# Two exchanges in the load queue of a causal-attention and feed-forward kernel on one core

## The chip, the cores and the metric

The kernel runs on one core of one Trainium2 chip. The metric is the device time of one execution in microseconds (us). The kernel before was run three times. The profile is of one further execution, and all times inside it count from the start of its span. The span goes from the first to the last instruction of the program; the device time is a little longer than the span.

## The reference

Inputs are q, k, v of shape (4 batches, 8 heads, 768 positions, 64), one decay factor lam for each head, and two float64 weight matrices: w_in (512 x 2048) and w_out (2048 x 512). The first half is linear attention with decay, in blocks of 64 positions:

```python
intra = einsum('bhic,bhjc->bhij', qb, kb) * Dmask      # Dmask: lam ** (i - j) for i >= j, else 0
intra = einsum('bhij,bhjd->bhid', intra, vb)
inter = einsum('bhid,bhde->bhie', qb * lam_pow, kv_state)
out[:, :, sl] = intra + inter
kv_state = lam_block * kv_state + einsum('bhsd,bhse->bhde', kb * rev_pow, vb)
```

The attention output, 3072 tokens of 512 features, goes through the second half:

```python
h = x @ w_in
g = maximum(0.01 * h, h)
return (g @ w_out).astype(float32)
```

## The kernel before

**Tiling.** The 3072 tokens are 24 chunks of 128 positions (6 chunks for each batch, two blocks of 64 in each chunk), and 4 chunks make a group of 512 tokens. The 2048 hidden features are 8 pairs of 2 x 128. For each group and each pair the kernel does an up projection (line 864) with its leaky ReLU on ScalarE (line 891), and stores the result to a scratch in DRAM (line 894). After the last group the down projection reads this scratch back (line 904) and multiplies by w_out (line 930). Each operand of these products is split into three float32r parts (h, l, m), and each product is made of three matmuls.

**One chunk of attention.** `load_kq` loads k and q, each in two DMAs of 128 KB (line 476), and `load_v` loads v in one DMA of 256 KB (line 538); both walk rows of 64 float32 numbers. `transposes` turns k and q with four TensorE transposes each (line 560), and ScalarE or VectorE copies them out of PSUM (line 541). k is then scaled in place by the decay (line 601). `scores` makes the kv products, which need k and v of the chunk, and the scores q k^T, with small 64 x 64 matmuls (line 420; in the trace they write psc, or banks called pt and b in the first four chunks). `outputs` makes scores times v and the first half of the inter-block product (48 small matmuls into po), then a tiny copy of two columns of po, called seen_po (line 692), then the scores of the next chunk, then the other half of the inter-block product (16 small matmuls into po). Those last 16 wait for seen_po. Then ScalarE writes the h part of the output (line 708) and VectorE the l and m parts (lines 716 and 734).

From chunk 8 on q is not transposed by TensorE: it is loaded in 16 blocks that are already put in place for VectorE's 32 x 32 transposes (`load_subs`, line 523, 32 KB for each block of chunks 8 and 9; `turn`, line 532).

**The weights.** `to_float32` loads half a pair of w_in as float64 words into one of three raw buffers, in two DMAs of 256 KB with rows of 2048 bytes (line 798), and makes float32 of it: three ScalarE instructions (lines 810, 812 and 814) and two of VectorE (lines 816 and 817). `parts` splits the pair into its parts wh, wm and wl (lines 823, 826 and 828).

**What sets the order.** Each step is recorded with `add` in a `Plan`, with its engine, a cost and the buffers that it reads and writes; it gets a number in the order of recording. `ORDER` (line 266) is a list of (number, engine) written out by hand, 1296 entries, that says in which order the recorded steps are emitted. Each engine then takes its own instructions in that order, and so does SyncE, which issues the loads one after the other. `Plan.emit` works out waits from the buffers that each step reads and writes.

```python
for i, e in self.order:
    if i < 0:
        done.append((free[e], len(done), i, e))
        free[e] -= 0.11 * i
        continue
    take(max(free[e], since(i, e)), i, e)
```

(A negative number asks for filler matmuls at that place; those stand early in the list.) Loads use few buffers: k, q and v have two each, taken by even and odd chunks, with extra places for chunks 2 and 3 (in buffers called gs and raw), and w_in rotates through three raw buffers.

The marker that orders the two halves of the inter-block product is recorded like this, and `ORDER` puts the one of chunk 7 on ScalarE, as (309, "ACT"):

```python
add(("DVE", "ACT"), (0.15, 0.25), lambda e: (nc.vector.tensor_copy if e == "DVE" else nc.scalar.copy)(seen_po, po[:, :, 0, 0]),
    ["po"], ["seen_po"], rank=-3.0)
between()
add("PE", 0.235, lambda: inter(1), needs + ["seen_po"], ["po"], kind="q")
```

The numbers that the change touches are 74 (load of v of chunk 3), 111 (two loads of q of chunk 4), 355 (two loads of w_in, second half of pair 7), 275 (one block of q for chunks 8 and 9) and 303 (load of v of chunk 8). The three conversions of the w_in half stand in ScalarE's order directly ahead of marker 309.

Of the kernel before, what the change touches and what calls it, by code (L numbers as in the profile page):

```python
# [239 lines left out]
def kernel(  # L240
# [127 lines left out]
    plan = Plan(kinds, also, {"k@2": early[0], "v@2": early[0], "k@3": early[1], "v@3": early[1], "q@3": early[2]})  # L368
    plan.fill, plan.idle, plan.warm, plan.order = busy, None if ORDER else busy, 1.3 + 0.22 * WARM, ORDER
    add = plan.add  # L370
# [686 lines left out]
```

## Time and profile before

| what | us |
|---|---|
| three runs | 608.04, 606.27, 607.43 |
| median | 607.43 |
| the profiled execution | 606.49 |
| its span | 604.7 |
| TensorE matmul busy | 595.9 |
| TensorE weight loads busy | 492.0 |
| VectorE busy | 294.4 |
| ScalarE busy | 209.2 |
| GpSimd busy | 70.0 |

In the profile PE is TensorE's matmuls, PEld its weight loads, DVE VectorE, ACT ScalarE, POOL GpSimd, and SPq SyncE's queue, which issues the loads. A row of the timeline has the start, the length, the engine, the line of the kernel, the operation, and what it writes and reads (att, gs, raw, po and so on are the names of the tiles; in_q_dram and the like are the inputs); a bracket at its end tells how long the engine was idle before it and what released it. A row of the waits has who waited for what, the sum, how often, and the longest. The length of an issue in SyncE's queue is not the time of the transfer: the landing comes later and has its own row, in us from issue to landing. The ends of matmuls are modelled, so a short wait can hide behind them.

### The profile page before, as it was taken

Reading aid. Unit: us, or ns where it says so; the run is one execution under the profiler, and the core shown is the slowest. Engines: PE = TensorE matmul, PEld = TensorE weight load, DVE = VectorE, ACT = ScalarE, POOL = GpSimd, SP = SyncE. Lnnn points to the kernel's source line nnn. Section 1 sums busy time; section 2 is a strip of 40 time slices with the busy share of each in tenths; the row PEclk is TensorE's granted clock in tenths of the full one; section 3 lists DMA queues with packets and bytes.
Section 4 is the critical chain, followed back from the end, with each engine's and each line's share of the span. In section 5 each row is a group of like instructions: output and inputs, shape, how many; then the busy total and the mean of one; then the engine's idle time right before and its main releaser. Section 6 shows DMA issues by size and latency. Waiting matters only on the chain.

```text
span 604.7 us, 12740 instructions
## 1 busy us (share of the span) xinstructions
PE 595.9 (99%) x5362; PEld 492.0 (81%) x5362; DVE 294.4 (49%) x410; ACT 209.2 (35%) x323; POOL 70.0 (12%) x84
## 2 busy tenths in 40 slices
PE   8899999999999999999999999999999999999997
PEld 5788888888888888887888888888888888888886
DVE  6798754450554434244167755354353543534430
ACT  4686651212433433435334421222312313214111
POOL 2311232241322031140000000000000000000000
PEclk9999999999999999999999999999999999999999
DMA  9998887597788788664975823433333333423201
GB/s 208 226 266 224 224 241 199 88 258 188 214 227 210 224 241 232 183 203 181 327 258 184 302 105 128 151 99 134 116 116 128 118 126 122 125 102 124 85 1 69
DMA packets 150249, 105.18 MB, mean 174 GB/s; under 512 B 126128, under 2 KB 126896, under 8 KB 150192
## 3 DMA queue, kind: packets, MB, share of 16 engines
q1 hardware_dynamic: 148848, 104.03, 58.6%
q8 instruction: 42, 0.69, 0.5%
q10 hardware_dynamic: 1344, 0.33, 0.2%
q14 instruction: 15, 0.12, 0.1%
HBM read 68.69 MB, written 35.65 MB: 173 GB/s over the span
## 4 chain that ended last, share of the span: by engine, by line
PE 95%; DMA 2%; SPq 1%; issue 0%; ACT 0%; DVE 0%; DVEq 0%; ACTq 0%
PE b L864 32%; PE b L930 16%; PE pt L864 11%; PE psc L930 11%; PE po L930 11%; PE pt L930 5%; PE po L420 4%; PE psc L420 3%; DMA att<-in_v_dram 2%; DMA att<-in_q_dram 1%; PE b L560 0%; PE po L560 0%; SPq L798 0%; PE b L420 0%; PE b L359 0%
## 5 line engine op out<-in xcount | busy, mean ns | idle before, releaser
L912 DVE SCALAR_TENSOR_TENSOR xl<-att,xh 128x1024 fp32r<-128x1024 f32 x48 | 58.7, 1223 | 125.8 <-ACT xh L911 125.8
L911 ACT ACTIVATE xh<-att 128x1024 fp32r<-128x1024 f32 x48 | 50.9, 1061 | 147.5 <-PE po L930 73.0
L864 PE MATMUL b<-xl,wl 128*128 128x512 f32 (+1 forms) x292 | 77.1, 388 | 0.0
L864 PE MATMUL b<-xh,wh 128*128 128x512 f32 (+1 forms) x292 | 76.5, 389 | 0.6 <-ACT wh L823 0.6
L864 PE MATMUL b<-xm,wm 128*128 128x512 f32 (+1 forms) x292 | 76.0, 390 | 0.0
L891 ACT ACTIVATE gs<-b 128x512 f32<-128x512 f32 x72 | 42.1, 597 | 96.3 <-PE b L864 87.1
L864 PEld LDWEIGHTS b<-xh,wh 128*128 128x128 f32 x292 | 53.9, 188 | 11.8 <-ACT wh L823 0.7
L864 PEld LDWEIGHTS b<-xl,wl 128*128 128x128 f32 x292 | 54.1, 188 | 11.2
L864 PEld LDWEIGHTS b<-xm,wm 128*128 128x128 f32 x292 | 53.8, 188 | 11.2
L914 DVE SCALAR_TENSOR_TENSOR xm<-xl,xh 128x1024 fp32r<-128x1024 f32 x48 | 58.8, 1226 | 4.7
L930 PE MATMUL b<-wh,xh 128*128 128x512 f32 x144 | 56.0, 389 | 0.0
L930 PE MATMUL b<-wl,xl 128*128 128x512 f32 x144 | 56.0, 389 | 0.0
L930 PE MATMUL b<-wm,xm 128*128 128x512 f32 x144 | 56.0, 389 | 0.0
L663 POOL TENSOR_TENSOR att<-att 128x256 f32<-128x256 f32 x40 | 27.8, 694 | 113.9 <-DVE att L660 66.2
L930 PE MATMUL psc<-wm,xm 128*128 128x512 f32 (+1 forms) x100 | 38.2, 387 | 0.0
L930 PE MATMUL po<-wm,xm 128*128 128x512 f32 (+1 forms) x100 | 37.9, 384 | 0.0
L930 PE MATMUL psc<-wh,xh 128*128 128x512 f32 x96 | 37.3, 389 | 0.0
L930 PE MATMUL psc<-wl,xl 128*128 128x512 f32 x96 | 37.3, 389 | 0.0
L930 PE MATMUL po<-wh,xh 128*128 128x512 f32 x96 | 37.3, 389 | 0.0
L930 PE MATMUL po<-wl,xl 128*128 128x512 f32 x96 | 37.3, 389 | 0.0
L420 PEld LDWEIGHTS po<-att 64*64 64x64 f32 x1408 | 27.0, 134 | 10.5 <-issue 7.8
L420 PE MATMUL po<-att 64*64 64x64 f32 x1408 | 33.0, 222 | 1.7 <-issue 0.9
(106 smaller groups left out, 860.5 us busy)
## 6 DMA issues: line engine op xcount, KB each, us to landing
att<-g SPq DMA_DIRECT2D x48, 512.0 KB, 3.4
g<-gs SPq DMA_DIRECT2D x47, 512.0 KB, 3.6
raw<-in_moe_w_in_dram SPq DMA_DIRECT2D x32, 256.0 KB, 4.3
raw<-in_moe_w_out_dram SPq DMA_DIRECT2D x16, 512.0 KB, 4.6
out_dram<-gs SPq DMA_DIRECT2D x23, 256.0 KB, 2.1
att<-in_v_dram SPq DMA_DIRECT2D x22, 256.0 KB, 3.8
att<-in_k_dram SPq DMA_DIRECT2D x43, 128.0 KB, 3.9
wo<-w SPq DMA_DIRECT2D x8, 512.0 KB, 4.0
```

Of the source, the lines that this page charges most:

```text
L420: nc.tensor.matmul(dst[HALF[cols]], lhsT=lhsT[HALF[rows]], rhs=rhs[HALF[rows]], start=start, stop=True, skip_group_check=True)
L663: add("POOL", 0.62, lambda new=new, j=j: behind(("s", j), nc.gpsimd.tensor_tensor(state[(j + 1) % 4], new, _bc(lam_c, 2, D), op=ALU.mult)) ...
L864: nc.tensor.matmul(dst, lhsT=w[z][:, kk * 2 * P + f * P:kk * 2 * P + (f + 1) * P], rhs=x[z][:, kk, toks], start=start and kk == 0, stop=kk ...
L891: add("ACT", ns, lambda b=b, r=r: nc.scalar.activation(out=r(), in_=b(), func=AF.Prelu, bias=0.0, scale=1.0, alpha=0.01), [kb], [kg], rank ...
L911: add("ACT", 1.05, lambda: nc.scalar.activation(out=h, in_=graw[j], func=AF.Copy, bias=0.0, scale=NEAR), reads, wr("h"))
L912: add("DVE", 1.215, lambda: nc.vector.scalar_tensor_tensor(l, graw[j], 1.0, h.bitcast(F32), op0=ALU.mult, op1=ALU.subtract), reads + [f"rh ...
L914: add("DVE", 1.215, lambda: nc.vector.scalar_tensor_tensor(m, l.bitcast(F32), -S, h.bitcast(F32), op0=ALU.mult, op1=ALU.add), [f"rh{j}", f ...
L930: nc.tensor.matmul(to[:, cols], lhsT=ring[j][z][:, f * T + tb * P:f * T + (tb + 1) * P], rhs=W[pp][z][:, f * d_model:(f + 1) * d_model][:, ...
```

## The change

Only the list `ORDER` is changed. The entry of q of chunk 4 (111) moves nine places forward, to stand just ahead of v of chunk 3 (74). Further on, v of chunk 8 (303) moves forward past the w_in load (355), and the q block (275) with it, so that the three go out as 303, 275, 355 where they went out as 355, 275, 303. The diff, cut to the entries about it (the list is one line in the code):

```diff
-    (98, "ACT"), (44, "ACT"), (74, "DMA"), (41, "POOL"), (45, "PE"), (54, "ACT"), (55, "DVE"),
-    (99, "DVE"), (100, "DVE"), (75, "PE"), (57, "DVE"), (111, "DMA"), (58, "PE"), (46, "ACT"),
+    (98, "ACT"), (44, "ACT"), (111, "DMA"), (74, "DMA"), (41, "POOL"), (45, "PE"), (54, "ACT"),
+    (55, "DVE"), (99, "DVE"), (100, "DVE"), (75, "PE"), (57, "DVE"), (58, "PE"), (46, "ACT"),
...
-    (282, "DMA"), (304, "DMA"), (355, "DMA"), (288, "ACT"), (275, "DMA"), (207, "POOL"),
+    (282, "DMA"), (304, "DMA"), (303, "DMA"), (275, "DMA"), (355, "DMA"), (288, "ACT"), (207, "POOL"),
...
-    (439, "DVE"), (293, "DVE"), (303, "DMA"), (357, "ACT"), (300, "POOL"),
+    (439, "DVE"), (293, "DVE"), (357, "ACT"), (300, "POOL"),
```

In SyncE's queue, which is the only one whose order changes, this reads (each line one step, "x2" for two DMAs):

```diff
 L798 raw<-in_moe_w_in_dram x2
+L476 att<-in_q_dram x2
 L538 gs<-in_v_dram
-L476 att<-in_q_dram x2
 L798 raw<-in_moe_w_in_dram x2
...
 L476 att<-in_k_dram x2
-L798 raw<-in_moe_w_in_dram x2
-L523 att<-in_q_dram
 L538 att<-in_v_dram
+L523 att<-in_q_dram
+L798 raw<-in_moe_w_in_dram x2
 L894 g<-gs
```

2 lines of the change are left out of this document (1 added, 1 removed).

## The prediction

> **What bounds the kernel now.** I read the page first, then the waits of TensorE, then its order of time around the places that those waits name, then the chain of work that ended last, and last the load queue and ScalarE at the same places.
>
> ```profile
> span 604.7 us, 12740 instructions
> ...
> PE 595.9 (99%) x5362; PEld 492.0 (81%) x5362; DVE 294.4 (49%) x410; ACT 209.2 (35%) x323; POOL 70.0 (12%) x84
> ```
>
> TensorE is busy 595.9 of 604.7 us, so 8.8 us is all that any reordering could win without making TensorE's work shorter, and this change does not touch that work. TensorE's waits name both places of the change:
>
> ```profile
> PE b L560 <- DMA att<-in_q_dram: 0.6, 1, 0.6
> ...
> PE psc L420 <- DMA att<-in_v_dram: 0.5, 1, 0.5
> ```
>
> The first is the transpose of q of chunk 4, the second the kv product of chunk 8. Together they are 1.1 us. The rest of the span is told by three stretches (columns: stretch, its length, busy time of PE, PEld, DVE, ACT, POOL, clock, DMA share, GB/s):
>
> ```profile
> 20.00:42.00 22.00, 20.77 (x452) 17.99 (x455) 19.30 (x33) 15.17 (x28) 6.17 (x7) 1.00 1.00 258
> ...
> 66.00:70.00 4.00, 3.47 (x137) 2.99 (x135) 2.62 (x6) 2.71 (x6) 1.06 (x1) 1.00 0.99 310
> 70.00:604.70 534.70, 531.27 (x4094) 439.62 (x4092) 238.97 (x306) 165.77 (x248) 52.01 (x56) 1.00 0.55 166
> ```
>
> From 70 us on TensorE has no listed wait, so whatever it gains or loses before 70 us arrives at the end one for one. And from 20 to 42 us the DMA engines are busy all the time (share 1.00): a load there lands when the bytes ahead of it are done, not when it was issued.
>
> **The change part by part.** No instruction is added or removed, and TensorE, VectorE, ScalarE and GpSimd keep their order. In SyncE's queue the two loads of q4 step ahead of the load of v3, and further back v8 and one block of q step ahead of the two loads of the second half of w_in of pair 7. So the cost is in landings alone.
>
> *First exchange.* TensorE at this place, the chain at the same place, and the two issues:
>
> ```profile
> 24.27 0.64 PE L864 MATMUL b<-xh,wh 128*128 128x256 f32 x4
> 25.55 0.95 PE L560 MATMUL b<-att 128*128 128x128 f32 x4 [0.64 <-DMA att<-in_q_dram]
> ...
> 26.89 0.27 PE L420 MATMUL pt<-gs 64*64 64x64 f32 x1
> ```
> ```profile
> 20.64 5.37 DMA att<-in_q_dram
> ...
> 26.05 0.44 PE b L560 x2
> ```
> ```profile
> 19.48 0.43 SPq L538 DMA_DIRECT2D gs<-in_v_dram  x1
> 20.01 1.45 SPq L476 DMA_DIRECT2D att<-in_q_dram  x2
> ```
>
> The second load of q4 lands at 20.64 + 5.37 = 26.01. TensorE loses 0.64 us before the first two transposes and, since four take 0.44 x 2 = 0.88 by the chain's row for two, under 0.3 us more before the last two: 0.9 us in all. One load of v costs the queue about 1.2 us (below, v8). Taken from ahead of q4 it lets q4 land at about 24.8, before TensorE is free at 24.91. So this wait goes. What is late next is v3: with the same bytes queued it lands where q4 did, at 26.01. Its reader is the kv product of chunk 3 (26.89), which would come at 26.89 - 0.9 = 26.0 and so starts at about 26.1. **Gain here: 0.8 us.**
>
> It does not last. The next loads are in the old order behind the same bytes, and v5 is already just in time:
>
> ```profile
> 40.56 0.86 PE po L420 x48
> 41.42 0.02 issue
> 41.44 1.09 PE psc L420 x44
> ```
> ```profile
> 36.62 0.59 SPq L538 DMA_DIRECT2D att<-in_v_dram  x1
> ```
> ```profile
> DMA to landing us min/median/max: 4.7/4.7/4.7
> ```
>
> v5 lands at 36.62 + 4.7 = 41.3; the product that reads it starts at 41.44. From v8's landing at 64.17 + 3.5 = 67.7 to its product at 67.84 it is the same 0.14 us. So at 41.44 TensorE is being let go by v5, although the list of waits shows nothing there, because the 48 matmuls ahead have modelled ends. If v5 does not land sooner, TensorE waits there for what it won at 26 us. Bounds of what survives: 0 (the landing stays) and 0.8 us (every later load moves along with TensorE). With a DMA share of 1.00 up to 42 us there is no idle DMA time to move into: I take **0**.
>
> *Second exchange.* The load queue, and behind it what each row took from issue to landing, in the same order (k9, w_in, q block, v8):
>
> ```profile
> 60.43 0.93 SPq L476 DMA_DIRECT2D att<-in_k_dram  x2
> 61.46 2.19 SPq L798 DMA_DIRECT2D raw<-in_moe_w_in_dram  x2
> 63.70 0.42 SPq L523 DMA_DIRECT2D att<-in_q_dram  x1
> 64.17 0.45 SPq L538 DMA_DIRECT2D att<-in_v_dram  x1
> ```
> ```profile
> DMA to landing us min/median/max: 3.7/3.8/3.9
> ```
> ```profile
> DMA to landing us min/median/max: 3.8/4.1/4.3
> ```
> ```profile
> DMA to landing us min/median/max: 2.8/2.8/2.8
> ```
> ```profile
> DMA to landing us min/median/max: 3.5/3.5/3.5
> ```
>
> Landings: k9's second load about 60.9 + 3.7 = 64.6; w_in 61.46 + 3.8 = 65.3 and about 62.0 + 4.3 = 66.3; the q block 66.5; v8 67.7. Their steps are 0.7, 1.0, 0.2 and 1.2 us, without a hole from 64.6 to 67.7. In the new order the same steps give v8 at 65.8, q at 66.0, w_in at 66.7 and 67.7. If 0.3 of w_in's step of 1.0 was its late issue (its twin took 0.7), it is 67.4. So v8 comes 1.9 us sooner, and **w_in 1.1 to 1.4 us later**. Who waits for w_in is ScalarE:
>
> ```profile
> 66.37 0.70 ACT L810 ACTIVATE w<-raw 128x512 f32<-128x512 f32 x1 [2.77 <-DMA raw<-in_moe_w_in_dram]
> 66.97 0.76 ACT L812 ACTIVATE low<-raw 128x512 uint16<-128x512 uint32 x1
> 67.61 0.77 ACT L814 ACTIVATE low<-raw 128x512 f16<-128x512 f32 x1
> 68.24 0.14 ACT L692 COPY att<-po 128x2 f32<-128x2 f32 x1
> 69.30 0.60 ACT L708 ACTIVATE xh<-po 128x512 fp32r<-128x512 f32 x1 [0.92 <-PE po L420]
> ```
> ```profile
> 66.38 0.93 PE L420 MATMUL po<-att 64*64 64x64 f32 x48
> 67.84 1.16 PE L420 MATMUL psc<-att 64*64 64x64 f32 x64 [0.53 <-DMA att<-in_v_dram]
> 68.79 0.44 PE L420 MATMUL po<-att 64*64 64x64 f32 x16
> ```
>
> ScalarE starts 0.07 after the landing and does three conversions in a row. Queued behind them stands the tiny copy of line 692 (the marker seen_po), and the last 16 matmuls of chunk 7, in TensorE's queue, wait for that marker. It is done at 68.38, 0.41 before those matmuls start at 68.79. Without the wait for v8 they would be ready at 68.79 - 0.53 = 68.26, so even with w_in untouched TensorE could gain only 68.79 - 68.38 = 0.41 us here. With w_in 1.1 to 1.4 later the marker ends at 69.5 to 69.8, and the 16 matmuls start 1.1 - 0.41 = 0.7 to 1.4 - 0.41 = 1.0 us later than now, some hundredths more for the release. **A wait of about 1.4 us takes the place of the 0.5 us one.** All that reads their result (line 708, the eviction, the up projection) moves along with TensorE.
>
> The Trainium skill, page "DMA: Bandwidth & Descriptors", section "Anatomy of one DMA — SWDGE (gpsimd) path", fits a DMA's moving part as bytes over 436 GB/s (for the other descriptor path). By it v8 (256 KB) and the q block (32 KB) would set w_in back by an estimated 0.7 us and the loss would be 0.3 us. The rows differ: v8's step alone is 1.2 us.
>
> *Sum.* 0 from the first exchange, 0.9 us lost at the second (between 0.7 and 1.0, rounded up for the release). The profiled execution took 606.49 us (span 604.7 and 1.8 around it), so it would be 607.4; it lies 0.94 below the median of the runs shown, 607.43. On the median the forecast is **608.3 us**.
>
> **The rivals.**
>
> *A, both waits simply go.* For it: each exchange hits a listed wait, and SyncE itself waits for TensorE now and then, so later loads may be issued sooner. Against: the full DMA engines, and the marker's place in ScalarE's order. It needs w_in's second load to land by 66.3 as now, and v5 0.8 sooner. It gives -0.8 and -0.41, about -1.2: 606.2.
>
> *B, the other way and larger: w_in's issue stalls.* One of the two w_in issues lasted 2.19 - 0.45 = 1.7 us instead of about 0.45, and landed about 2.6 after that issue ended (63.65 to 66.3). I assume that this stall stays at its time, about 62.0, where the q block is issued in the new order. If it goes with the w_in load instead, w_in's second issue ends at about 64.6 + 1.3 = 65.9 and lands near 68.5 to 68.9, 2.2 to 2.6 late: the 16 matmuls lose 1.8 to 2.2 us. It decides from an issue that ends after 65.1, as then the landing is later than the 67.7 of the queue. Against: the q block is issued first, and would take the stall. 609.4.
>
> *C, the change does not do what it says.* The gain at 26 us dies at v5, and w_in comes only a little later, by as much as the marker's slack of 0.41 or the 0.7 us of its bytes: 0 to +0.3, 607.6.
>
> **How the numbers follow.** Forecast 0.50, A 0.15, B 0.20, C 0.15. The range reaches to A and B: 606.2 to 609.6, the upper end being B's 609.4 and the 0.2 that its price is unsure of; what is left out is larger forms of A and B and a median that falls apart from this one. A median of this kernel cannot tell less than about 0.3%, 1.8 us, from no change (the three runs lie 1.8 apart). Faster by over that needs more than all the waits of A: 0.08, for A with a low median. Slower by over it: B and a few hundredths of the forecast, 0.26. Within it: 0.66.
>
> **What the profile of the changed kernel would show.** First exchange: no wait of line 560 near 25 us, the kv product of chunk 3 starting at about 26.1, and the product at 41.44 no sooner than now, with a gap before it of up to 0.8 in place of 0.02. Second: v8 landing near 66, no wait for it; ScalarE's line 810 starting at 67.5 to 67.8 in place of 66.37; the 16 po matmuls at about 69.5 to 69.8 with a listed wait for line 692. I am wrong if the product of v5 starts well before 41.4 (then the first gain survives), if line 810 starts near 66.4 (A or C), or if it starts after 68.3 (B). If the span changes with none of these moved, the cause is one that I have not seen.

## The result, and the profile after

The changed kernel took 608.24 us (median of 22 runs, 606.42 to 613.55), the kernel before 607.07 us beside it (22 runs, 606.08 to 608.91). The ratio is 1.0031, with a 95% interval of 1.0016 to 1.0046: slower by a little over 0.3%. The forecast was 608.3.

The middle hides two groups of runs. In 16 of the 22 TensorE's mean granted clock (the clock that it was given, 1.0 being full speed) is 0.999 or 1.0, and their mean time is 607.86 us. In the other six it is 0.994 to 0.997, and their mean is 612.08. The 22 runs of the kernel before have a mean of 607.07. So the difference of the means, 609.01 - 607.07 = 1.94 us, is 0.79 us in runs at full clock and 6/22 x (612.08 - 607.86) = 1.15 us from six runs at a lower clock. The profiled execution (612.42 us, span 610.6) is one of the six, so it shows both.

**First place.** TensorE's order in time in the changed kernel (start, duration, engine, line, and in brackets the idle time ahead with what ended it):

```profile
25.33 0.60 PE L560 MATMUL b<-att 128*128 128x128 f32 x4
...
26.33 0.27 PE L420 MATMUL pt<-gs 64*64 64x64 f32 x1
...
38.40 0.66 PE L560 MATMUL pt<-att 128*128 128x128 f32 x4 [0.23 <-ACT gs L891]
...
40.18 0.69 PE L560 MATMUL po<-att 128*128 128x128 f32 x4 [0.19 <-ACT low L814]
40.80 0.93 PE L420 MATMUL po<-att 64*64 64x64 f32 x48
41.96 1.09 PE L420 MATMUL psc<-att 64*64 64x64 f32 x46 [0.23 <-DMA att<-in_v_dram]
```

The same 48 matmuls (po, line 420) in the kernel before:

```profile
40.49 0.93 PE L420 MATMUL po<-att 64*64 64x64 f32 x48
```

The transposes of line 560 wait no more, and the kv product of chunk 3 starts at 26.33 in place of 26.89, 0.56 us sooner. v3, its input, lands at 20.13 + 5.9 = 26.03. One execution beside one other tells little here, though: e2, e8 and e10 below leave the first exchange out, line 560 does not wait in their profiles either, and the same product starts at 25.83, 25.99 and 25.55. The lead is gone before v5 is reached: the 48 matmuls ahead of its product start at 40.80 (40.49 before), behind the two short waits for ScalarE in the rows. The product itself starts at 41.96 (41.44 before), 0.18 us after v5's landing at 35.88 + 5.9 = 41.78.

**Second place.** The load queue (k9, v8, q block, w_in, the store of line 894), and what v8 and w_in took from issue to landing:

```profile
61.16 0.94 SPq L476 DMA_DIRECT2D att<-in_k_dram  x2
62.15 2.31 SPq L538 DMA_DIRECT2D att<-in_v_dram  x1
64.51 0.57 SPq L523 DMA_DIRECT2D att<-in_q_dram  x1
65.18 0.87 SPq L798 DMA_DIRECT2D raw<-in_moe_w_in_dram  x2
66.15 0.38 SPq L894 DMA_DIRECT2D g<-gs  x1
```
```profile
DMA to landing us min/median/max: 5.0/5.0/5.0
```
```profile
DMA to landing us min/median/max: 4.5/4.6/4.6
```

The issue that lasted long is now v8's own: 2.31 us instead of 0.45. v8 lands at 62.15 + 5.0 = 67.15, w_in near 65.6 + 4.6 = 70.2. ScalarE in the same stretch:

```profile
70.29 0.66 ACT L810 ACTIVATE w<-raw 128x512 f32<-128x512 f32 x1 [5.97 <-DMA raw<-in_moe_w_in_dram]
70.86 0.77 ACT L812 ACTIVATE low<-raw 128x512 uint16<-128x512 uint32 x1
71.49 0.75 ACT L814 ACTIVATE low<-raw 128x512 f16<-128x512 f32 x1
72.10 0.14 ACT L692 COPY att<-po 128x2 f32<-128x2 f32 x1
```

The marker of line 692 depends on nothing that is late; it merely stands behind three conversions that wait for w_in. TensorE:

```profile
67.10 0.93 PE L420 MATMUL po<-att 64*64 64x64 f32 x48
67.85 0.65 PE L420 MATMUL psc<-att 64*64 64x64 f32 x32
68.87 0.69 PE L420 MATMUL psc<-att 64*64 64x64 f32 x32 [0.38 <-DVE att L532]
72.31 0.70 PE L420 MATMUL po<-att 64*64 64x64 f32 x16 [2.74 <-ACT att L692]
72.94 2.07 PE L864 MATMUL b<-xm,wm 128*128 128x512 f32 x4
74.81 1.91 PE L864 MATMUL pt<-xh,wh 128*128 128x512 f32 x4
```

The wait for v8 is gone, and one of 2.74 us for the marker has come. The 16 matmuls start at 72.31 in place of 68.79: 0.72 us of this TensorE already brought along (67.10 against 66.38 for the 48 ahead), 2.80 are new. The next rows show a second loss: four matmuls that took 1.19 us now take 2.07. The granted clock tells why. First two stretches of the changed kernel, then the same matmuls (from the 16 to the product that starts at 80.03 after, 73.85 before) in both kernels; the columns are the stretch, its length, busy time of five engines, clock, DMA share, GB/s:

```profile
71.36:78.18 6.82, 5.87 (x28) 4.64 (x29) 5.55 (x11) 5.10 (x10) 0.00 (x0) 0.50 0.70 175
78.20:80.00 1.80, 1.80 (x9) 1.50 (x8) 1.80 (x3) 1.51 (x3) 0.39 (x1) 1.00 0.84 290
```
```profile
72.31:80.03 7.72, 7.72 (x36) 6.14 (x37) 6.97 (x11) 5.75 (x9) 0.42 (x1) 0.62 0.75 198
```
```profile
68.79:73.85 5.06, 5.06 (x52) 4.17 (x44) 4.26 (x8) 3.89 (x6) 0.00 (x0) 1.00 0.90 262
```

The clock is 0.50 from 71.36 on, still inside the wait, and 1.00 again from 78.20. The same work takes 7.72 instead of 5.06 us: 2.66 more. Then 0.72 + 2.80 + 2.66 = 6.18, which is what TensorE is behind at that point (80.03 - 73.85), and the two spans differ by 5.9.

### The profile page after: what moved, and what is told of

Read it like the earlier page. It is cut to its first block, busy times and chain, and to the rows that moved or that the text cites. A ratio compares the mean times of both kernels' runs of the same rounds, so it can differ in the third digit from the quotient of the medians.

```text
span 610.6 us, 12741 instructions
## 1 busy us (share of the span) xinstructions
PE 599.1 (98%) x5362; PEld 494.1 (81%) x5362; DVE 294.8 (48%) x410; ACT 208.5 (34%) x323; POOL 70.0 (11%) x84
## 4 chain that ended last, share of the span: by engine, by line
PE 94%; DMA 3%; SPq 1%; ACT 1%; issue 0%; DVE 0%; POOL 0%; DVEq 0%; ACTq 0%; POOLq 0%
PE b L864 31%; PE b L930 16%; PE psc L930 11%; PE po L930 11%; PE pt L864 11%; PE pt L930 5%; PE po L420 4%; PE psc L420 3%; DMA raw<-in_moe_w_in_dram 2%; DMA att<-in_v_dram 1%; PE b L359 1%; SPq L538 1%; PE b L560 0%; ACT low L812 0%; PE pt L560 0%
## 5 line engine op out<-in xcount | busy, mean ns | idle before, releaser
L663 POOL TENSOR_TENSOR att<-att 128x256 f32<-128x256 f32 x40 | 27.7, 693 | 120.6 <-DVE att L660 69.8
```

The lines of the kernel that those rows point to most:

```text
L663: add("POOL", 0.62, lambda new=new, j=j: behind(("s", j), nc.gpsimd.tensor_tensor(state[(j + 1) % 4], new, _bc(lam_c, 2, D), op=ALU.mult)) ...
```

## The experiments

The theories. **T**: the late w_in costs because ScalarE's marker stands behind the conversions of this w_in; TensorE waits there, and when the wait is long its clock is halved for some microseconds. **Rival 1**: the first exchange costs. **Rival 2**: neither place has a price, the difference is spread. **Rival 3**, formed after the first four runs: the clock halves for a cause other than the wait. In the table "low" counts runs with a mean clock below 0.998, and the ratio is to the kernel before on the same chip (35, 31, 29 and 11 runs of it beside the four sets, two of these 106 low).

| kernel | median us | before us | ratio (95%) | low |
|---|---|---|---|---|
| after | 608.24 | 607.07 | 1.0031 (1.0016 to 1.0046) | 6 of 22 |
| e1 first exchange alone | 607.01 | 607.53 | 0.9995 (0.9980 to 1.0011) | 0 of 12 |
| e2 second exchange alone | 609.44 | 607.53 | 1.0029 (1.0008 to 1.0050) | 6 of 12 |
| e3 after, conversions late | 608.74 | 607.53 | 1.0025 (1.0008 to 1.0041) | 3 of 12 |
| e4 before, conversions late | 609.57 | 607.53 | 1.0036 (1.0022 to 1.0050) | 0 of 12 |
| e5 after, also behind xm | 608.26 | 606.77 | 1.0021 (1.0007 to 1.0035) | 0 of 12 |
| e6 before, also behind xm | 608.76 | 606.77 | 1.0029 (1.0017 to 1.0042) | 1 of 7 |
| e7 after, filler in the wait | 608.41 | 606.77 | 1.0026 (1.0014 to 1.0037) | 0 of 12 |
| e8 v8 past the q block only | 607.79 | 606.77 | 1.0010 (0.9998 to 1.0022) | 0 of 11 |
| e9 after, marker and L708 first | 607.28 | 606.40 | 1.0008 (0.9997 to 1.0018) | 0 of 12 |
| e10 before, marker and L708 first | 607.93 | 606.40 | 1.0021 (1.0010 to 1.0032) | 0 of 12 |
| e11 after, conversions not waiting | 606.28 | 606.40 | 0.9987 (0.9973 to 1.0000) | 0 of 11 |
| e12 after, w_in one later | 610.93 | 606.60 | 1.0069 (1.0047 to 1.0092) | 5 of 6 |

**e1, the first exchange alone**, and **e2, the second alone** (entries of ORDER, against the kernel before):

```diff
 e1
+(111, "DMA"), (74, "DMA"), (41, "POOL"),
-(74, "DMA"), (41, "POOL"),
...
-(57, "DVE"), (111, "DMA"), (58, "PE"),
+(57, "DVE"), (58, "PE"),
 e2
-(304, "DMA"), (355, "DMA"), (288, "ACT"), (275, "DMA"),
+(304, "DMA"), (303, "DMA"), (275, "DMA"), (355, "DMA"), (288, "ACT"),
...
-(293, "DVE"), (303, "DMA"), (357, "ACT"),
+(293, "DVE"), (357, "ACT"),
```

> The first exchange alone (q of chunk 4 ahead of v of chunk 3). Theory (the whole loss sits behind the late w_in load): no change, -0.3 to +0.3 us; the transposes near 25 us no longer wait, and by the product of v5 near 41.4 us TensorE is where it was. Rival 1 (the first exchange costs, since in the changed kernel's trace TensorE is 0.5 us later at that product): +0.5 to +1.2 us.

> The second exchange alone (v of chunk 8 and the q block ahead of w_in). Theory: the whole loss, +0.9 to +1.5 us in the median; line 810 on ScalarE starts 1.1 us or more later, the last 16 po matmuls of chunk 7 wait 1.4 us or more for line 692, and some executions, those with the longest wait, are 4 us and more slower with a lower granted clock. Rival 1: at most +0.3 us. Rival 2 (no price in the queue, the spread of the changed kernel is only noise): within 0.3 us and no wider spread than before.

The first alone cannot be told from no change; the second alone is as slow as the whole change, within its interval. e1's interval reaches up to 0.7 us, so a small price of the first exchange is not excluded by it alone; but the second is slow without the first, and Rival 1 is out as the cause. The profiled execution of e2 (606.64 us, clock 1.0) shows the new wait by itself; first TensorE, then ScalarE:

```profile
65.36 0.93 PE L420 MATMUL po<-att 64*64 64x64 f32 x48
66.11 1.11 PE L420 MATMUL psc<-att 64*64 64x64 f32 x64
68.65 0.46 PE L420 MATMUL po<-att 64*64 64x64 f32 x16 [1.43 <-ACT att L692]
69.04 1.20 PE L864 MATMUL b<-xm,wm 128*128 128x512 f32 x4
```
```profile
66.62 0.68 ACT L810 ACTIVATE w<-raw 128x512 f32<-128x512 f32 x1 [4.04 <-DMA raw<-in_moe_w_in_dram]
...
68.45 0.13 ACT L692 COPY att<-po 128x2 f32<-128x2 f32 x1
```

No wait for v8, and 1.43 us for the marker. Here the clock stays whole; in six other runs of this kernel it does not, and their median is 610.97 against 607.34 of the rest. The rest have a mean of 607.53, no more than the 607.46 of the kernel before beside them: in these 12 runs the loss is all in the six with a low clock, and the length of the wait by itself is not seen in the times.

**e3 and e4, the conversions late.** To take the marker from behind the conversions, these were moved behind the marker, behind L708 and behind the evictions that follow, with and without the exchanges; the two VectorE steps that go on with them (359, 360) went along:

```diff
-(352, "ACT"), (296, "POOL"), (356, "ACT"), (341, "PE"),
+(352, "ACT"), (296, "POOL"), (341, "PE"),
...
-(357, "ACT"),
...
-(358, "ACT"),
...
-(309, "ACT"), (359, "DVE"),
+(309, "ACT"),
...
-(313, "ACT"), (400, "DMA"), (342, "PE"), (360, "DVE"), (314, "DVE"), (198, "DVE"),
+(313, "ACT"), (342, "PE"), (264, "ACT"), (343, "ACT"), (347, "ACT"), (356, "ACT"), (357, "ACT"), (358, "ACT"), (400, "DMA"),
+(314, "DVE"), (359, "DVE"), (360, "DVE"), (198, "DVE"),
```

> Both exchanges, and ScalarE's three conversions of that half of w_in (with the two steps of VectorE behind them) put behind line 692, line 708 and the three evictions. Theory: the wait for line 692 goes and v8 no longer waits, so 0.3 to 0.7 us faster than before, with a narrow spread and the clock at 1.0. Rival 1: still +0.5 to +1.2 us slower. Rival 2: as the changed kernel.

> The kernel before with the same move on ScalarE and VectorE and no exchange of loads. Theory: v8 still lands late, so the wait of 0.5 us stays and the time is that of before, -0.2 to +0.3 us; it tells whether the move itself is worth anything. Rival 2: the same.

T's numbers were missed, in e4 too: 2.0 us over the kernel before, where -0.2 to +0.3 was expected. The marker's wait is gone in e3, but a row stands in its list of waits (us in total, times, longest) that no theory had:

```profile
PE b L864 <- DVE xm L734: 1.0, 1, 1.0
```

The move put 359 and 360 ahead of step 198 on VectorE, the xm part of chunk 7 (L734), so that xm now waited for the late conversions instead of the marker; e4 has the same wait. A repair that passes a wait on to the next queue is no test of T. What can be read from the pair is that with the marker out of the way the exchanges show no loss: 608.74 against 609.57. Why three runs of e3 still had a low clock its one profile (clock 1.0) does not show.

**e5 and e6, 359 and 360 behind xm as well.**

```diff
-(314, "DVE"), (359, "DVE"), (360, "DVE"), (198, "DVE"), (354, "DVE"), (294, "DVE"),
+(314, "DVE"), (198, "DVE"), (354, "DVE"), (294, "DVE"),
...
-(147, "DVE"),
+(147, "DVE"), (359, "DVE"), (360, "DVE"),
```

> Both exchanges; in ScalarE's list the three w_in conversions (L810, L812, L814) stand behind the marker L692, behind L708 and the three ScalarE steps that follow it; on VectorE their two followers now stand behind the xm step (L734) and three more, so that xm is not held as it was in e3. Theory T (the late w_in costs only because ScalarE's marker and then xm stand behind its conversions, and the long wait then halves TensorE's clock): no wait for L692, no wait of L864 for xm, every run at a granted clock of 0.999 or more, 606.5 to 607.6, no run above 609.5. Rival 2 (the exchanges have no price there, the difference is spread): no change against the kernel after, 608.2. Rival 3 (the clock halves for another cause, not for the wait at the marker): runs at 0.994 to 0.997 stay, a quarter of all, with times above 609.5.

> The same move of the conversions without the two exchanges, so that the move's own price is seen. T: 607.0 to 608.0, all runs at 0.999 or more; the wait for v8 (0.5 us) stays, so it is 0 to 0.8 us slower than e5. Rival 2: equal to e5 within 0.3 us. Rival 3: as T says here.

No wait for L692 or xm, and no run of e5 has a low clock, as T said; its time, 608.26, is not what T said, and neither is the 608.76 of e6. Rows of e5, TensorE and ScalarE:

```profile
66.10 1.16 PE L420 MATMUL psc<-att 64*64 64x64 f32 x64
67.08 0.41 PE L420 MATMUL po<-att 64*64 64x64 f32 x16
...
80.35 2.23 PE L864 MATMUL b<-xh,wh 128*128 128x512 f32 x8 [0.84 <-ACT gs L891]
```
```profile
75.19 0.79 ACT L812 ACTIVATE low<-raw 128x512 uint16<-128x512 uint32 x1 [1.66 <-DMA raw<-in_moe_w_in_dram]
...
79.70 0.60 ACT L891 ACTIVATE gs<-b 128x512 f32<-128x512 f32 x1 [1.94 <-DMA g<-gs]
```

The 16 matmuls follow without a gap. But the conversions now end at 71.6, the w_in buffers come free later, and the next w_in conversion starts at 75.19 (73.20 before). SyncE, whose next four issues of w_in need these buffers, spends 7.84 us on them (3.39 before), so the store of line 894 behind them goes out at 76.81 (74.42 before). The eviction at 79.70 waits until this store has landed, and TensorE at 80.35 waits for the eviction. e6 has the same wait, 0.91 us. So the move itself costs, and only the pair can be compared.

**e7, filler.** Three matmuls without use (six records in the trace) in front of the 16, so that TensorE is not idle while it waits:

```diff
-(406, "DMA"), (312, "PE"),
+(406, "DMA"), (-18, "PE"), (312, "PE"),
```

> Both exchanges, and in TensorE's list three matmuls of an identity (512, 512 and 128 columns, some 1.9 us at the full clock, their result unused) directly ahead of the 16 po matmuls that wait for the marker. The wait itself is not touched, only the idleness in it. T: no run under a granted clock of 0.998, so none of the times of 609.8 to 613.6 that six of 22 runs of the kernel after had; the usual wait of about 1.4 us is overfilled by 0.5 us, so the median is 607.8 to 608.9. Rival 3 (clock halves for another cause): a quarter of the runs stay at 0.994 to 0.997 and the median rises to 608.7 or more. Rival 2: median 608.2 + 0.5 to 1.9.

Three rows of TensorE and one of ScalarE:

```profile
66.51 1.11 PE L420 MATMUL psc<-att 64*64 64x64 f32 x64
67.55 2.21 PE L359 MATMUL pt<-att 128*128 128x512 f32 x6
69.69 0.46 PE L420 MATMUL po<-att 64*64 64x64 f32 x16
```
```profile
68.70 0.13 ACT L692 COPY att<-po 128x2 f32<-128x2 f32 x1
```

In this execution the filler outlasts the wait (the marker is there at 68.83, the 16 start at 69.69), so the median is no better. But none of 12 runs has a low clock, against 6 of 22 and 6 of 12 without filler: that speaks for the idle time as what halves the clock. (These 12 ran on another chip than e2, and the kernel after was not run beside them.) Rival 3 comes up again with e12 below.

**e8, v8 past the q block only**, still behind w_in:

```diff
-(355, "DMA"), (288, "ACT"), (275, "DMA"),
+(355, "DMA"), (288, "ACT"), (303, "DMA"), (275, "DMA"),
```

> Of the second exchange only the harmless half, and the first exchange not at all: v of chunk 8 goes ahead of the block of q, both stay behind the w_in load. v8 then lands about 0.2 us earlier (the q block's step), w_in is not set back. T: 607.0 to 607.8, as the kernel before; no run under 0.999; at most 0.2 us of the wait for v8 gone, the q block 1.2 us later, at 67.7. Rival 2: the same. Rival 3 (any earlier v8 halves the clock): runs at 0.997 or below appear.

No low clock appears. 607.79 lies inside the expected 607.0 to 607.8, but it is 1.02 us over the kernel before beside it, and the interval only just includes no change. Two rows of its profile:

```profile
67.75 0.69 PE L420 MATMUL psc<-att 64*64 64x64 f32 x32 [1.19 <-DMA att<-in_v_dram]
69.18 0.69 PE L420 MATMUL psc<-att 64*64 64x64 f32 x32 [0.74 <-DVE att L532]
```

v8 came no sooner in this execution: it landed at 63.44 + 4.2 = 67.6 (67.7 before). The q block behind it landed at 63.91 + 3.9 = 67.8 instead of 66.5, and half of the scores waited once more for VectorE, which turns this block (line 532). So the q block is not harmless there, and e8 does not tell what a sooner v8 costs.

**e9 and e10, conversions directly behind the marker and L708**, ahead of the evictions:

```diff
+(313, "ACT"), (356, "ACT"), (357, "ACT"), (358, "ACT"), (400, "DMA"),
...
+(147, "DVE"), (359, "DVE"), (360, "DVE"),
```

> Both exchanges; the three w_in conversions stand directly behind the marker L692 and behind L708 in ScalarE's list (in e5 they stood behind three evictions L891 more), their VectorE followers behind the xm step as in e5. Theory T (the price of the late w_in is the marker's place behind its conversions; the price left in e5 is a w_in buffer that comes free late, so that the next w_in loads wait, 75.19 in place of 73.20 for the next conversion): no wait for L692 and none for xm, all runs at a granted clock of 0.999 or more; the conversions start near 68.1 instead of 69.6, so the loss behind it is 0.5 to 1.5 us smaller than in e5: 0 to 1 us over the kernel before, and 0.5 to 1.0 under the same move without exchanges (e10). Rival 2 (no price in the queue): equal to e5 and to e10 within 0.3 us. Rival 3 (clock halves for another cause): runs at 0.997 or below.

> The same move without the exchanges. T: 0 to 1.5 us over the kernel before, slower than e9 by 0.5 to 1.0 us, since the waits for q4 and v8 stay. Rival 2: equal to e9 within 0.3 us.

Both numbers came as T expected: 0.88 us over the kernel before, and 0.65 under e10. What is left of the move's price is in e9's waits as `gs`:

```profile
PE b L864 <- ACT gs L891: 1.0, 1, 1.0
```

Three pairs now suggest what the two exchanges are worth once the marker does not stand behind w_in: e3 against e4 -0.83 us, e5 against e6 -0.50, e9 against e10 -0.65. In the kernel as it is they cost 1.2. In each pair the two intervals overlap, so no pair shows a gain by itself; all three have the same sign.

**e11** was meant to make w_in later still. Step 355 was put behind 440, which stands behind the conversions in ORDER:

```diff
-(355, "DMA"),
...
-(440, "DMA"),
+(440, "DMA"), (355, "DMA"),
```

> The kernel after with the same w_in load moved back by two more issues, behind a store-like copy of 512 KB (L894) and a k load of 32 KB. T: w_in lands 1.5 to 2.5 us later still, the listed wait for L692 grows to 3 to 4.5 us, TensorE's clock halves in more than half of the runs (0.997 or below) and the median is 610 to 613. Rival 2: median 608.2 plus or minus 0.6. Rival 3 (clock halves for another cause): the wait grows and costs its 1.5 to 2.5 us, 609.7 to 610.7, with a quarter of the runs at a lower clock as in the kernel after.

So the edit did something else than its expectation says: the three conversions come ahead of this load and take what their buffer held before, and this half pair of weights is not the right one. As an experiment it is sharper than the one meant: both exchanges, and no wait of ScalarE for w_in. ScalarE, then TensorE:

```profile
64.24 0.65 ACT L810 ACTIVATE w<-raw 128x512 f32<-128x512 f32 x1
...
65.43 0.76 ACT L814 ACTIVATE low<-raw 128x512 f16<-128x512 f32 x1
68.15 0.16 ACT L692 COPY att<-po 128x2 f32<-128x2 f32 x1 [1.97 <-PE po L420]
```
```profile
67.91 1.26 PE L420 MATMUL psc<-att 64*64 64x64 f32 x64
68.98 0.41 PE L420 MATMUL po<-att 64*64 64x64 f32 x16
```

606.28 us, ratio 0.9987, all runs between 604.53 and 606.51 and at full clock. With that one wait away the whole loss is away. It is no version to keep.

**e12, w_in later, done rightly**: behind the store of 512 KB (step 256), its conversions still behind it, every engine's order as in the kernel after:

```diff
-(355, "DMA"), (288, "ACT"),
+(288, "ACT"),
...
-(345, "PE"), (256, "DMA"),
+(345, "PE"), (256, "DMA"), (355, "DMA"), (356, "ACT"), (357, "ACT"),
```

> The kernel after with one more exchange: the same w_in load goes behind the copy of 512 KB (L894) that followed it; the conversions stay behind the load, and the order of every engine's instructions is that of the kernel after. The copy is twice v8's bytes, whose step in the queue was 1.2 us, so w_in lands up to 2.4 us later still. T: listed wait for L692 of 3 to 4.5 us where e2 had 1.4, TensorE's mean clock at 0.997 or below in more than half of the runs, median 609.5 to 612. Rival 2 (no price in the queue): 608.2 plus or minus 0.6. Rival 3 (the clock halves for another cause than the wait): the wait grows and costs its 1.5 to 2.4 us, 609.7 to 610.6, and a quarter of the runs have the lower clock, as in the kernel after.

610.93 us; five of six runs have a low clock. The profiled execution (609.93 us): the 16 matmuls, and the two stretches in which the clock falls and comes back; between them it is 0.50.

```profile
70.78 0.46 PE L420 MATMUL po<-att 64*64 64x64 f32 x16 [2.59 <-ACT att L692]
71.17 1.29 PE L864 MATMUL b<-xm,wm 128*128 128x512 f32 x4
72.27 1.91 PE L864 MATMUL pt<-xh,wh 128*128 128x512 f32 x4
```
```profile
72.00:72.30 0.30, 0.30 (x3) 0.20 (x2) 0.30 (x1) 0.30 (x1) 0.00 (x0) 0.69 0.95 218
...
75.30:75.60 0.30, 0.30 (x2) 0.28 (x1) 0.30 (x2) 0.30 (x2) 0.00 (x0) 0.62 0.84 157
```

The wait is 2.59 us, longer than e2's 1.43 but no longer than the 2.74 in the profile after, and less than the 3 to 4.5 that T expected. The share of low runs is 5 of 6, against 6 of 22 for the kernel after and 6 of 12 for e2 on the same chip, as T expected and Rival 3 did not. Rival 2's 608.2, give or take 0.6, is out. By these two rows (a mean of 0.69 over 0.3 us is about 0.19 us at half clock) the clock is halved from about 72.1 to 75.5, for 3.4 us, and from a point at which TensorE had worked again for 1.3 us.

No run here beats the kernel before with the reference's work done. e1 (0.9995) and e9 (1.0008) are the nearest.

## Why the prediction was right, and what it left out

**Bound.** TensorE is busy for 98% of the span after, 99% before; the time moved by its waits, as the argument supposed, and by its clock, which the argument did not have.

**First exchange, taken as 0: the number is shown, the path only in part.** e1 alone gives 0.9995, and e2 without it 1.0029 against 1.0031 for both. In the profile after, the wait of line 560 is gone and v3 lands at 26.03 (forecast 26.01). The product of v5 still starts within 0.2 us of v5's landing, as the forecast said. But v5 did not take the whole gain of 0.8 us: the lead was gone 1.2 us earlier, at the 48 matmuls, and what was left for v5 is a listed wait of 0.23 us. And the wait that the exchange was meant to remove is missing in three of six profiles without the first exchange (e2, e8, e10), so it was never a sure 0.6 us.

**Second exchange, the mechanism: shown.** "A wait of about 1.4 us takes the place of the 0.5 us one" is e2's row of 1.43 us. The 48 matmuls ahead start 1.02 us sooner in e2 than before (65.36 against 66.38); on the time scale of before, ScalarE's line 810 then starts at 67.64 and the 16 matmuls at 69.67, inside the forecast of 67.5 to 67.8 and of 69.5 to 69.8. e11 takes the wait of the conversions away and the loss with it; the pairs with the marker moved suggest a gain of 0.5 to 0.8 us in place of the loss.

**The size of the sum: near, for the runs at full clock.** Forecast 0.9 us; the means differ by 0.79 in those 16 runs. In e2 they differ by 0.07 in six runs, so this size rests on the kernel after alone. That 608.24 lies so near to 608.3 is in part luck: the forecast put 0.9 us on 607.43, the median of three runs, and what came is 1.17 us on 607.07, with low runs in it that the forecast did not have.

**The term that was missing: the clock.** The sum had no line for what a wait does beyond its length. Six of 22 runs have a clock below 0.998, and they carry 1.15 of the 1.94 us. The medians differ by less, 1.17 us, since most runs are not among them. In both profiles with a low clock the fall comes within this wait (after) or 1.3 us behind it (e12); e7 (idle time filled, none low) and e12 (w_in later, 5 of 6 low) fit. That the wait brings the low clock in these runs is well supported; that nothing else does is not shown. The profiled execution, 4 us above the forecast, is such a run; the upper end of the range, 609.6, was passed by six of 22 runs, though not by their median.

**Rival B, half right.** It held that a long issue could push w_in further. That happened in the profiled execution: w_in's conversions start at 70.29, past B's line of 68.3, and the 16 matmuls lost 2.8 us here, more than B's 1.8 to 2.2. By the prediction's own sign this execution is B and not the forecast; e2's is the forecast. But the long issue did not go with w_in or, as I had argued against B, with the q block. It was v8's own, 2.31 us, and delays all that is issued behind. In the profiles of e2 and e12 it is the q block's and the store's:

```profile
60.94 1.61 SPq L523 DMA_DIRECT2D att<-in_q_dram  x1
```
```profile
62.66 1.42 SPq L894 DMA_DIRECT2D g<-gs  x1
```

In e3, e5 and e9, which have the same order of loads, it does fall on w_in, as B supposed: the pair takes 2.05, 1.96 and 1.67 us, 0.87 in e2. So near 61 to 66 us it follows the time more than a load, and which load it meets differs from execution to execution. What it is was not settled.

**Rivals A and C.** A needed w_in not to be late and v5 to come sooner; neither holds. Even e11, where ScalarE does not wait for w_in, gains 0.13% (0.8 us) where A had 1.2 us. C's 607.6 would need a delay of w_in within the marker's slack; the row of 1.43 us is against it.

**What stays open**: why three runs of e3 and one of e6 have a low clock though the marker is free there, and two of 106 runs of the kernel before; what the long issue is; how long the wait was in the runs without a profile; why e8 is 1.02 us over the kernel before.

## What to carry to other kernels

Before a load is moved back in a queue, look not at its reader but at what stands behind its reader on the same engine: here a copy of 128 x 2 elements, itself ready, kept TensorE waiting. When a step is moved to get it out of the way, follow all its successors on each engine, and the buffers that it frees; each of the three moves here made a new wait of 0.8 to 1.0 us elsewhere. On a kernel that TensorE bounds, price a wait by its length and by the clock: compare the granted clock of all runs, not the one profile.

## What the runs showed of the hardware that was not expected

- **The clock halves at a wait that is shorter than three microseconds.** In a listed wait of 2.74 us (with 0.38 idle just ahead) the clock fell after 1.8 us and stayed at 0.50 for 6.82 us; a wait of 2.59 us was followed by 3.4 us at 0.50. The mean clocks of low runs are mostly 0.997 and 0.994: over a span of 605 us, 3.4 us at half speed make 1 - 1.7/605 = 0.997, and twice that 0.994. So the halving seems to come in pieces of 3.4 us, one or two at a time. The Trainium skill, page "TensorE: Matmul & The Clock Gate", section "Part 1: The HAM clock gate (the "warmup" mystery)", tells of a free-running window of about 3.4 us after which an idle TensorE is set to half its clock. The length of the pieces agrees; the waits here were 0.7 to 0.8 us shorter than the window. One kernel has a low clock in some runs and not in others; whether their waits differ is not known, since one run of each was profiled.
- **The halving can come after the wait.** In e12 TensorE resumed at 70.78 and the clock fell at about 72.1, so the rows that look slow are not the ones next to the gap.
- **One issue on SyncE can take 1.4 to 2.3 us instead of 0.45**, near 61 to 66 us in several kernels and on a different load each time. It is not the only place: v5's issue took 1.69 us at 35.88 in the profile after.
